# Ordering VectorE and ScalarE work on an event clock, and seven-product blocks for two experts, in an attention and mixture-of-experts kernel

## The chip, the cores and the metric

The kernel runs on one core of one Trainium2 chip. The metric is the device time of one execution in microseconds (us). The profile's span, from the first to the last instruction, is about 1.7 us shorter: the profiled execution of the kernel before took 382.7 us and has a span of 381.0 us. Before the change, three runs took 383.38 to 383.81 us, median 383.64.

## The reference, cut to what matters

```python
# attention: B=4, H=8, S=768, D=64; each query sees the last 128 keys and 4 "sink" keys
scores = scale * np.matmul(q, k.transpose(0, 1, 3, 2))
scores = np.where(is_sink | in_window, scores, -1e9)
a = np.exp(scores - max); a = a / (sum + 1e-9)
x = np.matmul(a, v)                      # reshaped to 3072 tokens x 512
# mixture: 4 experts, F = 1024, every token goes through every expert
p = domain_probs / (domain_probs.sum(-1, keepdims=True) + 1e-09)
for e in range(4):
    h = np.maximum(x @ w1[e], 0.0)       # 3072x512 @ 512x1024
    out += p[:, e:e + 1] * (h @ w2[e])   # 3072x1024 @ 1024x512
```

## The kernel before

TensorE (PE) is the engine that matters. The build program keeps an estimate of every engine's time, `t["pe"]`, `t["dve"]` and so on (DVE is VectorE, ACT is ScalarE), and emits the PE work whose operands it expects to be ready first. The order of every engine is then fixed in the compiled kernel.

Batch 0 is handled directly. The other three batches give nine pairs of 256 tokens, so 36 units of (pair, expert). The first layer of a unit takes one of two forms.

- A direct unit is 32 matmuls of 128x256 on TensorE.
- A fast unit is a seven-product (Strassen-Winograd) block: seven products P1 to P7 of eight 128x128 matmuls, 56 in all. It needs weight forms, token forms and more additions on VectorE.

The second layer of every pair is always done with seven products, which need "S forms" of the hidden tile from VectorE. `START` says from which batch an expert is fast: `{0: 2}` makes expert 0 fast from batch 2, which is six units. The hidden tiles `H` have six buffers.

```python
    SLACK = 1500
    START = {0: 2}
    ...
    def sooner(cols, *deps, rate=0.96):          # ScalarE or VectorE, decided when emitted
        a = max(t["act"], *deps) + 205 + cols / 1.2
        d = max(t["dve"], *deps) + 192 + cols / rate
        if a <= d:
            return "act", act(cols, *deps)
        return "dve", dve(cols, *deps, rate=rate)
    ...
        # attention output: od is in PSUM, the division by the sum is one VectorE multiply
        nc.vector.reciprocal(out=R, in_=od[:, :, :, D:DX])
        nc.vector.tensor_mul(o[...], od[:, :, :, 0:D], R.to_broadcast([P, 2, 2, D]))
    ...
        def emit_product(self):                  # one second-layer product: 16 matmuls at once
            ...
            if bank == 0:
                nc.scalar.copy(out={"P1": C11, "P6": C12, "P7": C22, "P4": C21}[m], in_=x)
            else:                                # P2 and P3
                nc.vector.tensor_add(C, C, x)
            ...
    while mix.more() or att.more():              # the main loop; now = t["pe"]
        ...
        while t["dve"] < now + SLACK and mix.chore():   # a chore is one S form on VectorE
            pass
        ...
        # choose the next PE work; its VectorE and ScalarE work is emitted with it
```

The softmax here doesn't subtract the row's maximum and nothing guards it: scores larger than these inputs give would overflow.

## Time and profile before

| | Before |
|---|---|
| Time, median of 3 | 383.64 us |
| Span of the profiled execution | 381.0 us |
| TensorE busy | 97% |
| VectorE, ScalarE busy | 71%, 29% |
| Matmuls of fast first-layer units | 336 |

The head of the profile page of the kernel before gives the span, and busy time, share of the span and instruction count by engine.

```profile
span 381.0 us, 8821 instructions
...
PE 368.7 (97%) x3730; PEld 298.5 (78%) x3742; DVE 268.9 (71%) x613; ACT 109.5 (29%) x226; POOL 73.0 (19%) x98
```

A busy PE says nothing of how fast it streams, so the next look is at the chain of waits, here for 278 to 290 us of the kernel before. Columns: start, length (both us), engine, tile, source line and number of instructions. Of the tile names, `hps` and `cps` are the PSUM tiles of a direct and of a fast first layer, `acc` the two PSUM banks of the second layer, `H` the hidden tile, `S` the S forms and `osb` the output; in attention `sps` are the scores, `aT` the exponentials, `od` the output in PSUM, `R` the reciprocal of the sum and `onat` the scaled output.

```profile
278.21 0.45 PE cps L893 x8
278.65 7.86 PE hps L788 x72
286.51 0.45 PE cps L893 x8
286.96 1.75 PE acc L1000 x16
```

Eight 128x128 matmuls of a fast product (`cps`) take 0.45 us, 56 ns each. Seventy-two 128x256 matmuls take 7.86 us, 109 ns each. The pieces follow one another without a gap: in this stretch nothing waits and TensorE streams. A direct unit therefore costs 32 x 109 ns = 3.50 us, a fast one 56 x 56 ns = 3.13 us.

The stretch table of the kernel before shows the stages. Its columns are the stretch, its length, then busy time and instructions by engine, the granted TensorE clock (1.00 is full speed), the DMA share and GB/s.

```profile
core 0: us, PE busy (x) PEld busy (x) DVE busy (x) ACT busy (x) POOL busy (x), PEclk, DMA share, GB/s
0.00:66.30 66.30, 59.42 (x548) 40.34 (x553) 42.65 (x111) 33.21 (x68) 34.74 (x54) 1.00 1.45 187
121.00:264.00 143.00, 142.92 (x1541) 119.97 (x1541) 117.06 (x271) 35.70 (x76) 17.50 (x21) 1.00 0.67 92
264.00:364.00 100.00, 100.00 (x1020) 90.82 (x1019) 73.87 (x154) 9.04 (x21) 0.00 (x0) 1.00 0.12 37
```

Loading and the first attention take the first 66 us. From 121 to 264 us attention and mixture run together. From 264 to 364 us only the mixture is left.

The groups that the change touches, from the list of instruction groups of the kernel before (line, engine, operation, tiles, shapes, count, busy us, mean ns of one, idle time before and its releaser):

```profile
L805 DVE SCALAR_TENSOR_TENSOR H<-hps,gates 128x512 bf16<-128x512 f32 x120 | 80.2, 684 | 6.0 <-PE hps L788 5.3
L575 DVE TENSOR_TENSOR onat<-od,R 128x256 bf16<-128x256 f32 x48 | 20.4, 425 | 1.7
L893 PE MATMUL cps<-xT,w 128*128 128x128 bf16 x96 | 7.3, 219 | 0.0
```

The gating of the hidden tile is VectorE's largest item, 120 x 684 ns. The attention scaling is 48 x 425 ns. The 219 ns of a matmul is its recorded duration, not its cost: the spacing above is.

The timeline of the end of the kernel before has the same columns as the chain, with the idle time before an instruction and its releaser in brackets.

```profile
372.78 0.37 ACT L1013 COPY osb<-acc 128x256 f32<-128x256 f32 x1 [3.12 <-PE acc L1000]
...
373.21 1.91 PE L1000 MATMUL acc<-wf,H 128*128 128x256 bf16 x16 [0.46 <-ACT osb L1013]
...
376.90 0.42 DVE L1017 TENSOR_TENSOR osb<-osb,acc 128x256 f32<-128x256 f32 x1 [3.29 <-PE acc L1000]
377.34 0.33 SPq L1026 DMA_DIRECT2D out_dram<-osb  x1
377.77 0.38 SPq L1032 DMA_DIRECT2D out_dram<-osb  x1
```

One product waits 0.46 us, beyond the modelled end of the matmul before it, for ScalarE's copy of the bank that both use. After the last addition two output transfers are issued, 0.43 us apart.

### The profile page before, as it was taken

The numbers are of one execution on the slowest core, as the hardware profiler recorded it, in microseconds if no ns is written. First come the engines' busy times: TensorE is split into PE (matmuls) and PEld (weight loads), VectorE is DVE, ScalarE is ACT, GpSimd is POOL, SyncE is SP. The second block draws the span as 40 slices with busy tenths as digits, with TensorE's granted clock in tenths as the row PEclk, the third lists the DMA queues.
The fourth block names the chain that finished last, engine by engine and source line by source line (L and its number), as shares of the span: only waits on it lengthen the run. The fifth ranks groups of instructions, "written<-read, shape, count | busy, mean of one in ns | idle before, by whom it ended". The sixth has DMA issues, their size and how long they took to land.

```text
span 381.0 us, 8821 instructions
## 1 busy us (share of the span) xinstructions
PE 368.7 (97%) x3730; PEld 298.5 (78%) x3742; DVE 268.9 (71%) x613; ACT 109.5 (29%) x226; POOL 73.0 (19%) x98
## 2 busy tenths in 40 slices
PE   7789999999999999999999999999999999999995
PEld 3567666666766788888888888889999999999984
DVE  5676665864345898887887689689596695784960
ACT  4656533755453202313312223321101001010000
POOL 7965114701832075010110000000000000000000
PEclk9999999999999999999999999999999999999999
DMA  9999999940997999226692121122021020110101
GB/s 159 169 183 202 210 210 173 147 47 0 133 182 131 210 135 152 44 72 72 92 202 54 29 84 29 30 84 55 2 86 28 29 70 15 67 33 0 57 2 55
DMA packets 110802, 35.56 MB, mean 93 GB/s; under 512 B 94260, under 2 KB 106132, under 8 KB 110764
## 3 DMA queue, kind: packets, MB, share of 16 engines
q0 software_dynamic: 77520, 17.31, 50.2%
q1 hardware_dynamic: 33244, 17.70, 20.7%
q8 instruction: 29, 0.48, 0.5%
q14 instruction: 9, 0.07, 0.1%
HBM read 40.45 MB, written 6.34 MB: 123 GB/s over the span
## 4 chain that ended last, share of the span: by engine, by line
PE 80%; DMA 13%; POOL 3%; DVE 1%; issue 1%; ACT 1%; DVEq 0%; ACTq 0%
PE hps L788 33%; PE acc L1000 29%; DMA w<-in_moe_w_dram 7%; DMA qkn<-in_k_dram 6%; PE acc L1053 6%; PE cps L893 5%; PE sps L515 3%; PE od L563 2%; POOL vx L211 1%; POOL qkn L145 1%; PE od L556 1%; PE tr L436 1%; ACT aT L526 0%; POOL w L223 0%; PE sinks L488 0%
## 5 line engine op out<-in xcount | busy, mean ns | idle before, releaser
L788 PE MATMUL hps<-xT,w 128*128 128x256 bf16 x1344 | 161.7, 273 | 0.4 <-ACT aT L526 0.2
L788 PEld LDWEIGHTS <-w 128*128 128x128 bf16 x1344 | 127.2, 98 | 20.0 <-issue 3.4
L805 DVE SCALAR_TENSOR_TENSOR H<-hps,gates 128x512 bf16<-128x512 f32 x120 | 80.2, 684 | 6.0 <-PE hps L788 5.3
L1000 PEld LDWEIGHTS <-H 128*128 128x128 bf16 x720 | 68.7, 98 | 9.0 <-issue 1.4
L526 ACT ACTIVATE aT<-sps 128x512 bf16<-128x512 f32 (+1 forms) x96 | 47.7, 564 | 71.0 <-PE sps L515 70.9
L1000 PE MATMUL acc<-w,H 128*128 128x256 bf16 x432 | 51.4, 273 | 0.0
L1053 PE MATMUL acc<-w,H 128*128 128x512 bf16 x180 | 43.5, 379 | 0.9 <-issue 0.5
L1013 ACT COPY osb<-acc 128x256 f32<-128x256 f32 x36 | 13.4, 372 | 98.3 <-PE acc L1000 96.6
L799 ACT ACTIVATE H<-hps 128x512 bf16<-128x512 f32 x47 | 28.0, 604 | 34.9 <-PE hps L788 34.7
L211 POOL DMA_DIRECT2D vx<-in_v_dram x24 | 21.3, 893 | 79.2 <-PE od L563 68.5
L1000 PE MATMUL acc<-wf,H 128*128 128x256 bf16 x288 | 34.4, 273 | 0.5 <-ACT osb L1013 0.5
L533 DVE TENSOR_TENSOR aT<-aT,mask 128x1024 bf16<-128x1024 bf16 (+1 forms) x36 | 23.1, 643 | 15.9 <-ACT aT L526 15.9
L1053 PEld LDWEIGHTS <-H 128*128 128x128 bf16 x192 | 18.1, 98 | 18.3 <-issue 0.9
L1000 PEld LDWEIGHTS <-S 128*128 128x128 bf16 x288 | 27.9, 98 | 3.1
L1063 DVE SCALAR_TENSOR_TENSOR osb<-acc,scale_t,osb 128x512 f32<-128x512 f32 x18 | 13.5, 749 | 17.2 <-PE acc L1053 17.2
L563 PE MATMUL od<-vx,aT 128*128 128x65 bf16 x352 | 20.7, 193 | 1.4 <-DVE aT L530 0.9
L145 POOL DMA_DIRECT2D qkn<-in_q_dram x22 | 19.9, 905 | 10.7 <-DMA w<-in_moe_w_dram 4.1
L145 POOL DMA_DIRECT2D qkn<-in_k_dram x22 | 20.0, 907 | 9.7 <-DMA w<-in_moe_w_dram 8.5
L575 DVE TENSOR_TENSOR onat<-od,R 128x256 bf16<-128x256 f32 x48 | 20.4, 425 | 1.7
L563 PEld LDWEIGHTS <-aT 128*128 128x128 bf16 x352 | 17.3, 97 | 3.8 <-DVE aT L530 1.5
L515 PE MATMUL sps<-qkT 64*128 64x128 bf16 (+1 forms) x256 | 17.3, 239 | 1.0 <-ACT qkT L181 0.6
L1000 PE MATMUL acc<-w,S 128*128 128x256 bf16 x144 | 17.2, 273 | 0.0
(92 smaller groups left out, 319.1 us busy)
## 6 DMA issues: line engine op xcount, KB each, us to landing
w<-in_moe_w_dram POOLq DMA_DIRECT2D x7, 1024.0 KB, 18.8
out_dram<-osb SPq DMA_DIRECT2D x24, 256.0 KB
gates<-gate_rows SPq DMA_DIRECT2D x36, 128.0 KB
vx<-in_v_dram POOLq DMA_DIRECT2D x24, 128.0 KB, 6.0
qkn<-in_q_dram POOLq DMA_DIRECT2D x22, 128.0 KB, 6.9
qkn<-in_k_dram POOLq DMA_DIRECT2D x22, 128.0 KB, 6.9
w<-in_moe_w_dram POOLq DMA_DIRECT2D x2, 512.0 KB, 8.9
qraw<-in_q_dram SPq DMA_DIRECT2D x2, 256.0 KB
```

Source lines behind the costliest of these rows:

```text
L145: nc.gpsimd.dma_start(out=both[:, i], in_=src[b, :, tb * P:(tb + 1) * P, :].rearrange("h p d -> p h d"),)
L211: nc.gpsimd.dma_start(out=vx[tb][:, :, 0:D], in_=v[b, :, tb * P:(tb + 1) * P, :].rearrange("h p d -> p h d"),)
L515: nc.tensor.matmul(sps[ph][:, c:c + nq * P], lhsT=T[pr, 1, hp, kb * P:(kb + 1) * P], rhs=T[pr, 0, hp, qb * P:(qb + nq) * P], start=True, s ...
L526: nc.scalar.activation(out=a[:, ph], in_=sps[ph][:, 0:w], func=AF.Exp, scale=scale)
L533: nc.vector.tensor_mul(a, a, m[:, None, :].to_broadcast([P, 2, w]))
L563: nc.tensor.matmul(od[:, qi, ph], lhsT=a[:, ph, c:c + P], rhs=vx[kb][:, 2 * hp + ph, 0:DX], start=(g == 0 and i == 0), stop=(i == len(term ...
L575: nc.vector.tensor_mul(o[:, :, hp].rearrange("p q (h d) -> p q h d", h=2), od[:, :, :, 0:D], R.to_broadcast([P, 2, 2, D]),)
L788: nc.tensor.matmul(h[:, i].rearrange("p (q n) -> p q n", q=2), lhsT=w1_sb[e][:, db, fb * P:(fb + 1) * P], rhs=xT[b, g][:, :, db], start=(i ...
L799: nc.scalar.activation(out=dst, in_=h, func=AF.Relu)
L805: nc.vector.scalar_tensor_tensor(out=dst, in0=h, scalar=0.0, in1=gate, op0=ALU.max, op1=ALU.mult,)
L1000: nc.tensor.matmul(x, lhsT=self.operand(b, g, e, m)[:, f], rhs=forms[e][m][:, f], start=(i == 0 and m in ("P1", "P2", "P5")), stop=(i == n ...
L1053: nc.tensor.matmul(op, lhsT=H[:, fb // QF, fb % QF, s], rhs=w2_sb[e][:, fb, :], start=(fb == 0), stop=(fb == NFB - 1),)
```

## The change

Its intent is to make 15 units fast instead of six, and to let VectorE and ScalarE carry that: their work is put in a queue with a ready time and a due time and emitted on one event clock, the attention scaling goes to ScalarE, and products are issued in pieces of four matmuls between other work. The core of the diff, with cuts:

```diff
-    SLACK = 1500
-    START = {0: 2}
+    START = {0: 1, 1: 2}
+    ONACT = 1
@@
+    pend = []
+    def later(engine, ready, slack, run):
+        pend.append((ready, ready + slack, engine, run))
+    def flush(until, once=False):
...
+                at = max(t[engine], min(x[0] for x in mine))
+                if at <= until and (best is None or at < best[0]):
+                    best = at, engine, min((x for x in mine if x[0] <= at), key=lambda x: x[1])
...
@@ attention output
-        nc.vector.tensor_mul(o[...], od[:, :, :, 0:D], R.to_broadcast([P, 2, 2, D]))
+            def multiply(engine):                 # for batches from ONACT on
+                for qi in range(2):
+                    for ph in range(2):
+                        nc.scalar.mul(o[:, qi, hp, ph * D:(ph + 1) * D], od[:, qi, ph, 0:D], R[:, qi, ph])
+                        at = act(D)
+                scaled(at)
+            later("act", at, 600, multiply)
@@ second-layer product: pieces of QF = 4 matmuls, P1 seeds the other bank
-            for i in range(n):
+            for f in range(QF):
...
-                    start=(i == 0 and m in ("P1", "P2", "P5")), ...
+                    start=(k == 0 and f == 0 and m in ("P1", "P5")), ...
...
+                if m == "P1":
+                    nc.scalar.copy(out=acc[1][:, 0:G], in_=x)
@@ main loop
-        while t["dve"] < now + SLACK and mix.chore():
-            pass
+        flush(now)
+        mix.tokens()
+        mix.chore()
```

Before, P1's result was copied out and P2's added to it on VectorE. Now ScalarE copies P1 into the bank of P2, and P2 accumulates on it, which saves nine VectorE additions. The two halves of a pair's output are also sent when each is complete, so only one transfer is left after the last addition.

Three more parts of the diff are not in this cut. The first-layer work of two units may now be interleaved by readiness, where the old order had fixed places for it. A product may start on one expert's hidden tile, where the old one waited until the tiles or forms of all four experts were on their way. And a fast unit now starts only when three PSUM banks are free at once, where the old code took them as it went.

## The prediction

> **What bounds it now.** TensorE's issue rate. The page's busy table gives PE 97%, DVE 71%, ACT 29%. The chain of waits shows eight 128x256 matmuls in 0.87 us (109 ns each) and eight 128x128 matmuls in 0.45 us (56 ns each); "TensorE: Matmul & The Clock Gate", section "Wait — 56ns, not 53.3ns?", gives the same 55-56 ns, so this is the streaming rate and no wait. From 264 to 364 us the stretch table shows PE busy 100.0 of 100 us. Start-to-start gaps beyond the streaming rate sum to about 11.5 us in the first 40 us (loads, first attention chains), about 2 us near 60-66 us, some 6 us afterwards (mostly ~0.1 us around score matmuls with 64 rows) and one 0.5-0.6 us wait in the tail at 373.2 us (the next product waits for ScalarE's copy). VectorE and ScalarE are off the critical path almost everywhere; reordering them can recover only early gaps.
>
> **What the change does.** (a) Seven-product first layer: 6 -> 15 (pair, expert) units: expert 0 from batch 1, expert 1 from batch 2. Direct unit: 32 x 109 ns = 3.50 us of PE; fast: 56 x 56 ns = 3.13 us. Nine units save 3.3 us. (b) One more filler matmul (+0.1 us); other matmul counts are unchanged. PE stream: -3.1 us. (c) VectorE, by counts times measured means: 9 more fast units add 9 x (4x0.69+0.70+0.69) = 37.3 us and remove 36 direct gatings (-24.6); output scaling for batches 1-3 leaves (-15.3), nine output additions leave (-3.8), weight and token forms, relus moved from ScalarE add about +15. Net +8 us, to ~277 us. (d) ScalarE: 144 new 128x64 scalings; "ScalarE: Activation LUTs", section "What ACT_TABLE_LOAD costs", gives 186 ns + 0.833 ns per column + 93 ns for a pointer operand, about 93 ns overlapped: estimate 0.2-0.25 us each, 29-36 us; with copies and relus ~110 -> 140-150 us. No trace yet shows the small form. (e) Second-layer products are issued in pieces of four matmuls, interleaved with other work; with free operands a switch costs nothing visible (fast to product switches at 265-302 us are gapless). (f) P1 now seeds the other accumulator through a ScalarE copy, and P2 waits for it. Mid-kernel, 1.3 us of other matmuls lie between. In the last pair nothing does: I expect new waits of about 0.3 us for the last gating and 0.6-0.7 us for the copy. Against that, one output transfer instead of two is issued after the last addition (the second came 0.43 us later): about -0.5 us.
>
> **Critical path.** -3.1 (PE stream) + 0.6 (tail) + about 0.3 (new waits in attention stretches where slower output scaling holds PSUM banks, less what better early ordering returns) = -2.2 us.
>
> **Predicted:** 381.4 us, range 379.3 to 383.8. Faster by over 2%: 2%; within 2%: 96%; slower by over 2%: 2%.
>
> **What would show it.** Right: PE still 97% or more; fast-layer matmuls 336 -> 840 at 56 ns spacing; a middle pair takes ~25.5 us instead of 25.8; DVE ~277, ACT 140-150 us busy; a new wait of PE for ScalarE's P1 copy just before the end; first-40-us gaps 10-12 us again. Wrong: PE idle in the 264-364 us stretch; the first 66 us changed by over 1.5 us.
>
> **What would make it wrong.** Real VectorE or ScalarE durations differing from those the fixed order assumes, so that a late small operation stalls PE repeatedly (+3 us or more); or the due-time order removing much of the early gaps (-3 us).

The two pages that it names by their titles are pages of the Trainium skill.

## The result, and the profile after

| | Before | After |
|---|---|---|
| Time, median of 4 runs each (range) | 383.73 us (383.38 to 384.50) | 381.02 us (380.10 to 381.50) |
| Span of the profiled execution | 381.0 us | 379.8 us |
| TensorE, VectorE, ScalarE busy (us) | 368.7, 268.9, 109.5 | 368.6, 271.6, 146.2 |

The ratio is 0.9924, with a 95% interval of 0.9899 to 0.9948, so the time is the same within 2%. Here and below a ratio is the mean time of one kernel's fast runs over that of the kernel before's fast runs of the same rounds, so it is not quite the ratio of the quoted medians. The profiled execution of the changed kernel was the slowest of its four (381.5 us), and that of the kernel before was faster than its median (382.7 us): the two spans differ by 1.2 us, less than the medians do.

The head of the page, after:

```profile
span 379.8 us, 9469 instructions
...
PE 368.6 (97%) x3959; PEld 299.5 (79%) x3959; DVE 271.6 (71%) x616; ACT 146.2 (39%) x383; POOL 72.9 (19%) x98
```

PE's busy time is the same although it streams less: a 128x128 matmul is recorded for 219 ns and the next one starts after 56, so the records overlap and their union hides both short waits and the rate. The Trainium skill, "Perfetto Trace Analysis", section "Identifying the Most-Contended Engine", says that matmul busy time is not a good measure of how close a kernel is to the peak rate, and this pair of pages agrees (368.7 and 368.6 us busy). So I use a sum of my own. Every matmul start is subtracted from the next; what exceeds the streaming interval of that shape (56 ns for 128 columns, 109 for 256, 216 for 512) is a wait, and the rest is the stream. By counts of matmuls the stream is 353.8 us before and 350.7 after, -3.1 us. The level depends on how the small matmuls that run side by side are counted; the difference does not.

Three pieces of the chain of waits after, from 290.94 us:

```profile
290.94 6.99 PE acc L1156 x64
297.93 0.89 PE cps L1016 x16
298.82 3.49 PE acc L1156 x32
```

The rates are those of before, 56 and 109 ns, and switching between fast products and pieces of second-layer products costs nothing. The stretch table after:

```profile
0.00:66.30 66.30, 60.81 (x551) 41.06 (x552) 46.80 (x121) 31.95 (x64) 34.16 (x53) 1.00 1.45 186
121.00:264.00 143.00, 141.82 (x1670) 120.37 (x1668) 111.96 (x256) 63.52 (x188) 18.26 (x22) 1.00 0.68 90
264.00:364.00 100.00, 100.00 (x1126) 92.09 (x1124) 76.29 (x160) 14.90 (x34) 0.00 (x0) 1.00 0.13 39
```

From 121 to 264 us VectorE has 5 us less to do and ScalarE 28 more. PE loses about 1 us there. The groups after:

```profile
L963 DVE SCALAR_TENSOR_TENSOR H<-hps,gates 128x512 bf16<-128x512 f32 x84 | 57.2, 685 | 4.6 <-PE hps L939 3.6 <-DMA gates<-gate_rows 0.7
L687 ACT ACTIVATE onat<-od,R 128x64 bf16<-128x64 f32 x144 | 33.2, 327 | 44.4 <-DVE R L675 44.3
L1016 PE MATMUL cps<-xT,w 128*128 128x128 bf16 x240 | 18.3, 219 | 0.0
```

The direct gatings fell from 120 to 84, and the fast products rose from 96 to 240 in this form (336 to 840 in all). The 144 new scalings cost ScalarE 327 ns each as recorded. The tail after, in the timeline:

```profile
364.72 0.36 ACT L1180 COPY acc<-acc 128x256 f32<-128x256 f32 x1 [6.41 <-PE acc L1156]
...
372.73 1.91 PE L1156 MATMUL acc<-wf,H 128*128 128x256 bf16 x16 [0.46 <-ACT osb L1189]
...
376.42 0.42 DVE L1184 TENSOR_TENSOR osb<-osb,acc 128x256 f32<-128x256 f32 x1 [3.29 <-PE acc L1156]
376.87 0.33 SPq L1186 DMA_DIRECT2D out_dram<-osb  x1
```

After ScalarE's copy of P1, the next product starts at 365.13 us, with 0.45 us of recorded idle time and 0.61 us in my sum: the new wait. The old one stands unchanged at 372.73. One transfer is left after the last addition. From the last matmul's start to the end of the span, 4.4 us became 3.7 us.

Lastly, the timeline of the largest new wait in the middle:

```profile
204.45 0.69 DVE L963 SCALAR_TENSOR_TENSOR H<-hps,gates 128x512 bf16<-128x512 f32 x1 [0.72 <-DMA gates<-gate_rows]
...
205.06 0.17 DVE L675 RECIPROCAL R<-od 128x4 f32<-128x4 f32 x1
...
205.27 0.93 ACT L687 ACTIVATE onat<-od,R 128x64 bf16<-128x64 f32 x4 [0.81 <-DVE R L675]
...
206.25 0.34 PE L583 MATMUL sps<-qkT 64*128 64x256 bf16 x4 [0.85 <-ACT onat L687]
```

Read it upwards. The scores on PE wait for a PSUM bank that ScalarE's scaling frees; the scaling waits for VectorE's reciprocal; that stands behind a gating, which waited 0.72 us for its row of gates. The wait is 1.02 us in my sum in this execution, 0.49 in another of the same kernel.

The waits by stage, in us, from the starts of the matmuls:

| Stage (us) | Before | After | After, second profile |
|---|---|---|---|
| 0 to 40 | 11.7 | 12.2 | 12.8 |
| 40 to 121 | 3.5 | 3.6 | 3.5 |
| 121 to 264 | 6.1 | 7.6 | 7.1 |
| 264 to 360 | 0 | 0 | 0 |
| 360 to the last matmul | 0.6 | 1.2 | 1.2 |

Twelve of the kernel before's 128x512 matmuls have no record, and I took their gaps out where they fall, which makes its column uncertain by some tenths. The first row varies by about 2 us between the profiles of all runs (about 11 to 13), whatever the edit.

### The profile page after: what moved, and what is told of

Read it like the earlier page. It is cut to its first block, busy times and chain, and to the rows that moved or that the text cites. A ratio compares the mean times of both kernels' runs of the same rounds, so it can differ in the third digit from the quotient of the medians.

```text
span 379.8 us, 9469 instructions
## 1 busy us (share of the span) xinstructions
PE 368.6 (97%) x3959; PEld 299.5 (79%) x3959; DVE 271.6 (71%) x616; ACT 146.2 (39%) x383; POOL 72.9 (19%) x98
## 4 chain that ended last, share of the span: by engine, by line
PE 74%; DMA 15%; DVE 4%; POOL 3%; ACT 2%; issue 1%; DVEq 0%; ACTq 0%
PE acc L1156 28%; PE hps L939 23%; PE cps L1016 11%; DMA w<-in_moe_w_dram 7%; DMA qkn<-in_k_dram 6%; PE acc L1226 6%; PE sps L583 3%; PE od L648 2%; DVE H L963 1%; ACT onat L687 1%; POOL vx L243 1%; POOL qkn L185 1%; DMA gates<-gate_rows 1%; ACT aT L608 1%; PE tr L484 1%
## 5 line engine op out<-in xcount | busy, mean ns | idle before, releaser
L939 PE MATMUL hps<-xT,w 128*128 128x256 bf16 x1056 | 131.4, 273 | 0.9 <-DMA w<-in_moe_w_dram 0.6
L939 PEld LDWEIGHTS <-w 128*128 128x128 bf16 x1056 | 99.4, 98 | 15.1 <-issue 1.6
L963 DVE SCALAR_TENSOR_TENSOR H<-hps,gates 128x512 bf16<-128x512 f32 x84 | 57.2, 685 | 4.6 <-PE hps L939 3.6
L1156 PE MATMUL acc<-w,H 128*128 128x256 bf16 x432 | 56.4, 273 | 0.4 <-ACT acc L1180 0.4
L687 ACT ACTIVATE onat<-od,R 128x64 bf16<-128x64 f32 x144 | 33.2, 327 | 44.4 <-DVE R L675 44.3
L1226 PE MATMUL acc<-w,H 128*128 128x512 bf16 x192 | 45.4, 379 | 0.0
L1016 PEld LDWEIGHTS <-w 128*128 128x128 bf16 x480 | 30.6, 98 | 1.7 <-issue 0.8
L1035 DVE SCALAR_TENSOR_TENSOR H<-cps,gates 128x512 bf16<-128x512 f32 x45 | 30.6, 682 | 0.1
L952 ACT ACTIVATE H<-hps 128x512 bf16<-128x512 f32 x35 | 21.3, 608 | 23.0 <-PE hps L939 22.9
L1044 ACT COPY cps<-cps 128x512 f32<-128x512 f32 x15 | 8.7, 582 | 44.1 <-PE cps L1016 44.1
L1016 PEld LDWEIGHTS <-vf 128*128 128x128 bf16 x360 | 22.5, 98 | 0.7 <-issue 0.2
```

The lines of the kernel that those rows point to most:

```text
L687: nc.scalar.mul(o[:, qi, hp, ph * D:(ph + 1) * D], od[:, qi, ph, 0:D], R[:, qi, ph])
L939: nc.tensor.matmul(h[:, i].rearrange("p (q n) -> p q n", q=2), lhsT=w1_sb[e][:, db, fb * P:(fb + 1) * P], rhs=xT[b, g][:, :, db], start=(i ...
L963: nc.vector.scalar_tensor_tensor(out=dst, in0=h, scalar=0.0, in1=gate, op0=ALU.max, op1=ALU.mult,)
L1016: nc.tensor.matmul(y[:, f], lhsT=A[:, d, f * P:(f + 1) * P], rhs=T[:, d], start=(m in ("P1", "P5") and f == 0 and d == 0), stop=(d == 1), ...
L1035: nc.vector.scalar_tensor_tensor(out=dst, in0=src, scalar=0.0, in1=gate, op0=ALU.max, op1=ALU.mult)
L1156: nc.tensor.matmul(x, lhsT=self.operand(b, g, e, m)[:, f], rhs=forms[e][m][:, f], start=(k == 0 and f == 0 and m in ("P1", "P5")), stop=(k ...
```

## The experiments

The prediction's account was that only the shorter stream and the tail pay, while reordering VectorE and ScalarE is neutral. Its rivals were that the new order itself recovers time, or that the order and the units are not separable: that the old order could not have carried 15 units. Twelve kernels were run, all correct, in four groups; each group shares its runs of the kernel before (medians 383.70, 382.99, 383.39 and 383.35 us). Ratios are to those.

### The new order with the old units

```diff
-    START = {0: 1, 1: 2}
+    START = {0: 2}
```

> The changed kernel with the seven-product form cut back to the 6 units of the kernel before (expert 0, batches 2 and 3). Theory A (the gain is the 9 added units' shorter matmul stream, and the due-time order itself is worth nothing): PE stream is within 0.1 us of before, so 383 to 385 us, ratio to before 0.999 to 1.003. Theory B (the due-time order and event clock made the gain, the units only ride along): about 381 us, ratio 0.992 to 0.995.

Measured: 382.88 us (381.99 to 385.00), ratio 0.9984 (0.9954 to 1.0014). Stream 353.9 us, as before. With the six old units everything else in the change (event clock, scaling on ScalarE, pieces, seeded P2, one transfer fewer) is worth nothing that five rounds can tell; the interval leaves room for 1.8 us of gain to 0.5 us of loss.

### The old order with the new units

This is the kernel before with only its constant changed.

```diff
-    START = {0: 2}
+    START = {0: 1, 1: 2}
```

> The kernel before with nothing changed but 15 seven-product units in place of 6. Theory A: the stream shrinks by 3.25 us and VectorE, in plain program order, still keeps up, so about 380.0 to 381.2 us, ratio 0.990 to 0.994. Theory B: the old emission order cannot feed the longer chains of two seven-product experts, VectorE runs late, and at least 2 us of the 3.25 is lost in new waits of TensorE: 382.5 us or more.

Measured: 391.69 us (390.45 to 392.15), ratio 1.0208 (1.0184 to 1.0232). The stream shrinks as in the changed kernel, and yet the time is 8 us longer. The waits from 121 to 264 us are about 14 us (6.1 before), and from 264 to 360 us 3.0 us (0 before). The timeline of this kernel shows both. First, attention of batch 2 with no mixture work beside it:

```profile
160.55 0.68 DVE L533 TENSOR_TENSOR aT<-aT,mask 128x1024 bf16<-128x1024 bf16 x1
...
161.29 0.30 PE L563 MATMUL od<-vx,aT 128*128 128x65 bf16 x4 [0.62 <-DVE aT L533]
...
163.40 0.41 DVE L958 TENSOR_TENSOR H<-H 128x512 bf16<-128x512 bf16 x1
```

The step waits 0.62 us for VectorE's mask, with nothing else to issue, and so does the next one, at 162.44 us. From 153.6 us PE issues no first-layer matmul for 19.2 us. The first product that uses S forms starts only at 162.75 us, against 149.5 us in the kernel before. In the old loop an S form goes to VectorE only while the clock has VectorE less than `SLACK` = 1.5 us ahead; a backlog stops the forms, the products wait for them, the six hidden tiles stay occupied, and no new unit can start. The trace bears this out: of the twelve S forms of the pair, ten have been started by 149.51 us, and the eleventh (`H<-H` above) starts only at 163.40. From 150 to 165 us VectorE is busy 14.69 us, mostly with attention and gatings.

Second, once per pair after 264 us:

```profile
289.17 0.42 DVE L958 TENSOR_TENSOR H<-H 128x512 bf16<-128x512 bf16 x1
...
290.44 0.68 DVE L917 TENSOR_TENSOR cps<-H,cps 128x512 f32<-128x512 f32 x1
...
291.18 0.61 PE L893 MATMUL cps<-T,w 128*128 128x128 bf16 x8 [0.56 <-DVE cps L917]
```

The P6 sum (L917), which the next fast product needs, stands on VectorE behind three S forms and a gating that were emitted earlier. PE waits 0.72 us in my sum (0.56 recorded). Both are waits for VectorE in its fixed order. Its total by stage is not the cause: from 264 to 364 us it is busy 76.95 us, and 76.29 in the changed kernel; from 121 to 264 us it is 116.98, and 117.06 in the kernel before.

### More units in the new order

```diff
-    START = {0: 1, 1: 2}
+    START = {0: 1, 1: 1}
```

> The changed kernel with expert 1 in the seven-product form from batch 1 as well: 18 units. Theory A: 3 more units at 0.366 us each, so 1.0 us under the changed kernel, about 379.5 to 380.3 us, ratio 0.989 to 0.991. Rival: VectorE is nearly full around batch 1 (forms of weights are still being made there), and the three units gain nothing or lose: 381 us or more.

Measured: 388.69 us (388.33 to 390.00), ratio 1.0141 (1.0117 to 1.0165). Three units more shorten the stream by another 1.0 us, and the time grows by about 8. The number is where the rival had put it, but VectorE turned out not to be the reason. The stretch table of this kernel:

```profile
140.00:144.00 4.00, 2.66 (x35) 1.77 (x31) 1.66 (x4) 4.00 (x20) 4.00 (x6) 0.74 2.30 152
144.00:148.00 4.00, 3.36 (x40) 2.22 (x39) 1.66 (x4) 4.00 (x14) 3.53 (x5) 0.50 2.02 148
148.00:152.00 4.00, 4.00 (x32) 3.19 (x30) 1.46 (x3) 3.90 (x13) 0.00 (x0) 0.50 2.82 150
```

Between 131.9 and 148.2 us no first-layer matmul is issued. In the fixed order, the first fast unit of expert 1 in batch 1 is due; its P1 needs three free PSUM banks at once, and attention steps keep taking the banks one by one. ScalarE is then busy all the time (8.00 of the 8 us from 140 to 148) and seems to set the pace. On top of that, PE's granted clock falls to 0.50 at about 141.9 us and stays there to 152 us. The Trainium skill, "TensorE: Matmul & The Clock Gate", section "A second HAM failure mode: psum-queue depth-cycling", tells of a kernel whose PE idles briefly between groups of matmuls, through cycling of PSUM, so often that its clock goes back and forth between half and full. This trace agrees in part: PE was recorded busy for 2.40 of the 4 us from 138 to 142, up to the drop, with no idle gap over 0.61 us, and eight 128x128 matmuls then took 1.04 us as recorded instead of 0.61. But here the clock fell once and came back once.

### No fast units in the new order

```diff
-    START = {0: 1, 1: 2}
+    START = {0: 4}
```

> The changed kernel with no seven-product unit at all, so every unit is direct. Theory A: 6 units fewer than before, 2.2 us more stream than before: about 385.5 to 387 us, ratio 1.005 to 1.009; the four points 0, 6, 15, 18 lie on one line of 0.366 us per unit. Theory B: below the kernel before, 383 us or less.

Measured: 385.91 us (384.49 to 386.62), ratio 1.0057 (1.0033 to 1.0080). By counts its stream is 356.1 us. From 0 to 6 units the time falls by 3.0 us for a stream shorter by 2.2; from 6 to 15 by about 2 us (the changed kernel ran in other groups) for 3.2. Within the noise of about 1 us a unit is worth what its matmuls say, 0.37 us, or somewhat less at the upper end, until at 18 units another limit takes over.

### The changed kernel again, as control

No edit. It ran in one group with the next three.

> The changed kernel itself, as the partner of the three other runs of this call. 380.1 to 381.5 us again, ratio to before 0.991 to 0.994.

Measured: 380.99 us (380.39 to 381.74), ratio 0.9948 (0.9930 to 0.9967), just above the ratio expected, as the kernel before ran a little faster in this group.

### The last pair without the seed

In the last pair P1 is copied out and P2 added, as before; the others keep the seed.

```diff
-   start=(k == 0 and f == 0 and m in ("P1", "P5")), ...
+   start=(k == 0 and f == 0 and m in (("P1", "P2", "P5") if (b, g) == PAIRS[-1] else ("P1", "P5"))), ...
+                if plain and m == "P1":
+                    nc.scalar.copy(out=C11, in_=x)
+                    acc_free[0] = act(G)
+                    return
+                if plain and m == "P2":
+                    nc.vector.tensor_add(C11, C11, x)
+                    acc_free[1] = dve(G)
+                    return
```

> In the last pair alone, P2 starts a sum of its own as in the kernel before, instead of waiting for ScalarE's copy of P1 into the other accumulator; VectorE adds the two. Theory: the 0.61 us gap of TensorE at 365 us is that wait, and nothing else hides there, so the kernel is 0.5 to 0.6 us shorter than the control. Rival: the gap is the wait for the last gating (VectorE ends it at 365.04 us), and TensorE only waits for it a few matmuls later: 0.1 us or less.

Measured: 379.97 us (379.20 to 380.95), ratio 0.9921 (0.9903 to 0.9939). The waits after 360 us are 0.61 us instead of 1.21, so the wait for the P1 copy is gone and nothing took its place. In its timeline the last eight matmuls of P1 and the sixteen of P2 are now one group without a gap:

```profile
362.72 2.78 PE L1156 MATMUL acc<-w,H 128*128 128x256 bf16 x24
```

The 0.6 us is shown in the trace; the timed difference from the control, 1.0 us by the medians, has overlapping intervals.

### The DMA transposes paced

A block's transposes are issued only when the DMA queue is free, so that the gate rows do not stand behind them.

```diff
-        if turns and not mix.second and ...
+        if turns and t["sp"] < now + 300 and not mix.second and ...
```

> The transposing loads of batch 3 are put on the DMA queue one at a time instead of five in a row, so that gate rows are not held behind 10 us of them. Theory: the 1.0 us gap of TensorE at 206 us begins with a gate row that lands late (VectorE waits 0.72 us for it, then reciprocal, scaling and the bank of the scores follow late); it disappears, and the kernel is 0.7 to 1.0 us shorter than the control. Rival: the gap comes from the four slow scalings on ScalarE; then it stays, and the time is that of the control within 0.3 us.

Measured: 380.56 us (379.48 to 381.15), ratio 0.9933 (0.9914 to 0.9953). The wait near 206 us is 0.20 us instead of 0.49 in the control (0.42 to 1.02 in three profiles without this edit). That is the direction expected, but the wait did not disappear, and the effect is too small for the times to tell it.

### Attention scaling on VectorE

```diff
-    ONACT = 1
+    ONACT = 4
```

> Attention output of all batches scaled on VectorE by one instruction (as before the change) instead of four small ones on ScalarE for batches 1 to 3. ScalarE loses 33 us, VectorE gains 36 x 0.425 = 15 us busy time. Theory C (scaling on ScalarE costs TensorE waits, as the chain shows ScalarE's scaling before the 1.0 us gap): 0.5 to 1.3 us shorter than the control. Theory D (VectorE is the scarcer engine and the move pays): 0.5 us or more longer. Theory E (both engines have slack in those stretches): equal within 0.4 us.

Measured: 380.12 us (379.19 to 381.30), ratio 0.9925 (0.9905 to 0.9945). VectorE is busy 280.4 us and ScalarE 118.7. The wait near 206 us is gone, and so are two waits of 0.33 us, at 215.0 and 244.5 us in the changed kernel, where ScalarE's output copy stood behind four scalings. The waits from 121 to 264 us are 6.7 us (control 7.1). So the move to ScalarE isn't needed and costs some tenths in the trace; the intervals of the times overlap. The Trainium skill, "ScalarE: Activation LUTs", section "Rules for kernel authors", says to use VectorE for multiplications; here one VectorE multiply takes 0.42 us and the four ScalarE scalings that replace it 0.93 us, which agrees in direction, though the page speaks of the cost per element and here one instruction stands against four. VectorE has room for it, with 9 us more to do than in the changed kernel.

### The old order with a longer leash

If the S forms starve because of `SLACK`, a larger one must help.

```diff
-    SLACK = 1500
-    START = {0: 2}
+    SLACK = 3000
+    START = {0: 1, 1: 2}
```

> The kernel before with 15 seven-product units (391.7 us) and one number changed: the second layer's forms may be put on VectorE's queue while it is up to 3.0 us behind TensorE, not 1.5. Theory F (in the old order the forms starve under VectorE's backlog, the six hidden-tile buffers fill, and the attention of batch 2 runs alone for 19 us): the stretch without first-layer matmuls falls from 19 to under 8 us, TensorE's waits from 121 to 264 us fall by 5 us or more, and the time is 384 to 387 us; the 0.7 us waits once a pair after 264 us stay or grow, for the forms still stand before the chain's additions. Rival (VectorE simply has too much work there for any order): 390 us or more.

Measured: 384.74 us (384.10 to 385.38), ratio 1.0041 (1.0021 to 1.0061). The longest stretch without a first-layer matmul between 121 and 264 us falls from 19.2 to 6.6 us, and the waits after 264 us from 3.0 to 0.2 us. The stretch table from 121 to 264 and from 264 to 364 us, first with `SLACK` 1500 and then with 3000:

```profile
121.00:264.00 143.00, 137.78 (x1584) 115.80 (x1583) 116.98 (x269) 39.27 (x83) 18.23 (x22) 1.00 0.68 90
264.00:364.00 100.00, 97.79 (x1096) 89.31 (x1094) 76.95 (x160) 13.47 (x30) 0.00 (x0) 1.00 0.13 37
```

```profile
121.00:264.00 143.00, 139.63 (x1626) 118.14 (x1625) 120.47 (x276) 39.29 (x83) 18.09 (x22) 1.00 0.66 89
264.00:364.00 100.00, 99.90 (x1130) 91.95 (x1129) 80.39 (x167) 14.55 (x32) 0.00 (x0) 1.00 0.15 42
```

Some 7 us come back with this one number, so `SLACK` was the main cause of the 8 us. The account in theory F is only half confirmed. From 121 to 264 us the waits fell by about 3 us (14 to 11.0), not by 5 or more, and the waits after 264 us, which were expected to stay or grow, nearly vanished; why a longer leash removes those too was not looked into. The kernel is still some 4 us above the changed one. Longer leashes were not tried, so whether the old order could be brought all the way by this number stays open.

### The event clock without due times

Among the operations that are ready, the one that became ready first is taken, not the one due first.

```diff
-   best = at, engine, min((x for x in mine if x[0] <= at), key=lambda x: x[1])
+   best = at, engine, min((x for x in mine if x[0] <= at), key=lambda x: x[0])
```

> The changed kernel, but each engine takes the operation that became ready first instead of the one due first; everything else stands. Theory G (the due times are what keeps the seven-product chains fed: an addition with slack 0 passes forms with slack 3000 and weight forms with slack 9000): 0.5 us or more of waits in each late pair and more in the attention stretches, 383 us or more. Rival H (it is enough that an operation is put in the queue only when its input is ready on the event clock; due times add nothing): 380.5 to 382 us, within 0.3% of the changed kernel.

Measured: 380.68 us (379.87 to 380.81), ratio 0.9930 (0.9909 to 0.9951). Due times are worth nothing here. What is left of the queue is that an operation is put on its engine only once its inputs are there on the clock, so that by the estimate nothing waits at the head of an engine's order for work that comes later. That this is what gives the 4 us over the longer leash is argued and not shown: the pieces of four matmuls, the two units open at once and the three banks taken together also differ between the two kernels, and no run takes them out one by one.

### Eighteen units, with banks kept for them

While a fast unit waits for its three banks and attention is not behind, attention may start no new step.

```diff
+        def starting(self):
+            ...
+                    return max(self.T_at[b, g], forms1_at[e]) <= t["pe"] < free_at(3)
@@
+            if not due and mix.starting():
+                opts = [o for o in opts if o[3] != "todo"]
```

> The 18-unit kernel (388.7 us) with one rule added: while a seven-product unit waits for its three PSUM banks and attention is not behind its schedule, no new score tiles are begun. Theory I (the 18-unit kernel lost because attention kept taking the banks that the unit needs three of at once, so TensorE had nothing but the attention chain for 16 us): the stretch without first-layer matmuls falls from 16 to under 9 us and the time to 379.3 to 380.5 us, at or below the changed kernel. Rival (VectorE has no room for three more units in batch 1): 384 us or more.

Measured: 380.75 us (380.00 to 381.35), ratio 0.9937 (0.9916 to 0.9958). The stretch of 121 to 150 us in the two 18-unit kernels, without and with the rule:

```profile
121.00:150.00 29.00, 24.97 (x286) 18.02 (x285) 20.12 (x47) 20.98 (x71) 15.52 (x19) 0.86 1.72 164
```

```profile
121.00:150.00 29.00, 28.97 (x349) 23.37 (x346) 26.28 (x60) 12.52 (x36) 12.87 (x16) 1.00 1.66 158
```

PE issues 349 matmuls instead of 286 there, the clock is 1.00 again, and the longest stretch without a first-layer matmul from 121 to 264 us falls from 16.2 to 8.8 us. So attention beginning new steps while the unit waited for its banks was the cause of the 8 us, and with it the fall of the clock went too. The demand for three banks at once is the changed kernel's own rule; the old code did not have it. The time is 0.25 us above the range expected. The extra 1.0 us of stream is not seen as a gain over 15 units: the waits from 121 to 264 us are 8.3 us (control 7.1). Whether that is a limit of VectorE, of the banks or of this rule stays open.

### What pointed to a better version, together

The 15 units with the unseeded last pair, the scaling on VectorE and the paced transposes: the edits of those three runs in one kernel.

> The changed kernel with the three edits together that each came out at or below the control: last pair unseeded (measured gap 0.61 us), attention output scaled by one VectorE instruction (its run lay 0.2% below the control, and the waits at 206, 215 and 244 us, about 1.1 us together, were gone), transposing loads paced. If they add up: 1.2 to 1.8 us below the changed kernel, 379.0 to 379.8 us, ratio to before 0.988 to 0.990, so it beats both kernels. If they share one cause or were noise: 380 us or more, ratio 0.992 or more.

Measured: 379.91 us (379.26 to 380.39), ratio 0.9901 (0.9870 to 0.9932). It beats the kernel before by 1.0% and is by the medians about 1 us below the changed kernel, though it ran in another group than the control. It cannot be told from the unseeded tail or the VectorE scaling alone, so the three gains did not clearly add up.

## Why the prediction was right or wrong, point by point

1. **The time: right, in part by luck.** 381.02 us against 381.4, within the range. The 15 units pay through the stream, and the rest nearly cancels. That part is luck: the tail came out 0.7 us better than its term (point 4) and the attention stretches 0.7 to 1.2 us worse (point 3).
2. **The PE stream: right.** -3.1 us predicted and -3.1 us by the counts; 840 fast matmuls at 56 ns. A pair in the middle takes 25.5 us instead of 25.8, as predicted, and 264 to 364 us stayed full.
3. **Attention stretches: mis-sized.** The term "+0.3 (new waits in attention stretches ...)" measured +1.0 to +1.5 us from 121 to 264 us in the two profiles. The named mechanism, slower scaling holding banks, is there (the chain at 206 us) and the waits for ScalarE's output copy come to it; with the scaling on VectorE the stage falls by about 0.4 us, so it explains only a part. The rest was not found.
4. **The tail: half right.** The wait for ScalarE's P1 copy came as predicted, 0.61 us, and taking the seed out removed it. The wait "of about 0.3 us for the last gating" did not appear. By the code P1 reads only the first half of each hidden tile, and in pieces the last expert's turn comes late; no run tests this reason. The end shortened by 0.7 us, not 0.5. The tail as a whole gave -0.1 us where "+ 0.6 (tail)" stood in the sum, though its own text says 0.3 + 0.6 to 0.7 - 0.5, which is 0.4 to 0.5.
5. **ScalarE: right.** 146.2 us busy, predicted 140 to 150. The Trainium skill, "ScalarE: Activation LUTs", section "What ACT_TABLE_LOAD costs", gives the terms of an estimate, 186 + 0.833 x 64 + 93 = 332 ns for such a scaling; the trace has 327 ns. Four take 0.93 us from start to end, so they start (0.93 - 0.327) / 3 = 0.20 us apart.
6. **VectorE: right in direction.** 271.6 us busy, predicted 277. The sum added durations that overlap when operations follow at once (a 684 ns gating and the next one start 0.60 us apart), which is part of the 5 us.
7. **The step that failed** is "VectorE and ScalarE are off the critical path almost everywhere; reordering them can recover only early gaps". It is true of the kernel before, and the run with six units shows no gain from the new order there (0.9984, interval 0.9954 to 1.0014). It is false as an account of the change. With 15 units the old order loses 8 us, and with the longer leash it is still 4 us behind the new one, so the reordering, taken as a whole, is what makes the 3.1 us reachable; which of its parts does it is not shown. I had taken a change's parts as addends; the profile before could show what the order costs at six units, and not what it would cost at 15. Nor did early gaps shrink: the first 40 us have 12.2 and 12.8 us of waits against 11.7.

The sum of the measured terms is -3.1 (stream), +0.5 (first 40 us, within its variation), +0.1 (40 to 121 us), +1.5 (121 to 264 us), +0.6 and -0.7 (tail), which is -1.1 us, near the 1.2 us between the two spans. The medians differ by 2.7 us. The difference is which executions were profiled; stage by stage, only the profiled ones can be seen.

## What to carry to other kernels

When a change moves an engine's work and at the same time changes how it is ordered, test the two apart before calling either neutral: a schedule that shows no cost at today's load can be the thing that breaks at tomorrow's. A limit on how much work may stand in the queue of an engine off the critical path can starve the work that frees buffers; here the bill showed on TensorE as an attention chain running alone for 19 us. Where one block needs several PSUM banks at once, as in the 18-unit kernel, see to it that single-bank work cannot go on taking them one at a time.

## What the Trainium skill lacked or had wrong

- "TensorE: Matmul & The Clock Gate", section "Back-to-back issue gap", gives a sustained spacing for pairs of weight load and matmul of about 81 ns at 128 columns and about 131 ns at 512. This kernel has a weight load for every matmul and runs at 56 ns for 128 columns (0.45 us for eight), 109 ns for 256, and 216 ns for 512, which is the spacing that the page gives for the isolated case.
- The same page, section "What's actually happening", has the clock fall after an idle window of about 3.4 us, and gives no share of busy time below which a window counts as idle. Here it fell to 0.50 at about 141.9 us of the 18-unit run, with PE recorded busy 2.40 of the 4 us from 138 to 142 and no idle gap over 0.61 us.
- "ScalarE: Activation LUTs", section "What ACT_TABLE_LOAD costs", gives an overlap of about 93 ns for activations back to back. The 128x64 scalings from PSUM with a pointer scale take 327 ns and start 0.20 us apart, an overlap of about 0.125 us.
- No page sets four small scalings on ScalarE beside one broadcast multiply on VectorE: 0.93 us against 0.42 us here.
